# Attention and MLP on one core: the output block in consecutive rows, both squares of an MLP bank together, bulk loads issued in every step

## The chip, the cores and the metric

The kernel runs on one core of one Trainium2 chip. The time is the device time of one execution in microseconds (us). The core has five engines that run at the same time and wait for each other through semaphores: TensorE (PE, with PEld for its weight loads), VectorE (DVE), ScalarE (ACT), GpSimd (POOL) and SyncE (SP). In this kernel SP does nothing but issue DMA transfers, all of them, in the order in which the program lists them. Sixteen DMA engines move the bytes between the HBM and SBUF, the on-chip memory. TensorE writes its results to PSUM banks, from which ACT and DVE read.

## The reference

```python
def reference(A_x, A_wqkv, A_wo, B_x, B_w1, B_b1, B_w2, B_b2):
    xn = _layernorm(A_x, axis=-1)                     # (1, 2048, 640)
    s = _A_ref(xn, A_wqkv, A_wo)
    g = _silu(_B_ref(xn, B_w1, B_b1, B_w2, B_b2))
    return A_x + s * g

def _A_ref(x, wqkv, wo):                              # 32 heads of 20, window 256
    qkv = (x @ wqkv).reshape(B, S, 3, H, Dh).transpose(2, 0, 3, 1, 4)
    q, k, v = qkv[0], qkv[1], qkv[2]
    scores = jnp.einsum("bhqd,bhkd->bhqk", q, k) * (Dh ** -0.5)
    idx = jnp.arange(S)
    mask = (idx[:, None] - idx[None, :] >= 0) & (idx[:, None] - idx[None, :] < W)
    scores = jnp.where(mask[None, None], scores, -1e9)
    p = _softmax(scores, axis=-1)
    o = jnp.einsum("bhqk,bhkd->bhqd", p, v)
    return o.transpose(0, 2, 1, 3).reshape(B, S, D) @ wo

def _B_ref(x, w1, b1, w2, b2):                        # 640 -> 1536 -> 640
    h = jnp.einsum("bsd,df->bsf", x, w1) + b1
    r = jnp.where(h > 0, h, 0)
    return jnp.einsum("bsf,fd->bsd", r * r, w2) + b2
```

## The kernel before

**Precision.** A product of two float32 matrices is made of three: each operand is split into a high part, that TensorE takes at full rate, and the rest (`hi`, `lo`), and hi·hi, hi·lo and lo·hi are added up in one PSUM bank.

**Stages.** In the first stage (to about 115 us) the input is normalized, transposed and kept both in SBUF (`xT`) and in memory (`xs_d`); v and the first group of q and k are computed and stored (`v_d`, `qk_d`). The second stage is a loop over 16 head pairs times 16 tiles of 128 rows, plus 11 steps to run out: 267 steps. In step s, for pair p = s // 16 and tile q = s % 16, `scores` makes a tile of scores and `maxima` takes its row maxima on DVE. Every fourth step (s % 4 = 0) `max_rows` transposes the maxima of four tiles, ACT and POOL turn them into two rows, and SP sends these to rows 60 and 61 of the `qs` tile (L503), from where they are subtracted inside the next product. Nine steps behind (`LAG`), `scores_t` makes the transposed scores with these rows (`stps`, L518), ACT takes the exponential, POOL masks. Eleven steps behind, `values` multiplies four tiles by v (`ops`, L546), whose 21st column is all ones and so gives the sum of the row; ACT copies the result to `osb` (L551), and SP stores it to `o_d` (128 KB: for each of two heads and for even and odd tiles 32 rows, of which 21 are used, by two tiles of 128 columns).

**The filler.** The attention leaves TensorE time in each step. It is filled by a generator, `filler`: the other groups of q and k (`qkps`), then the MLP in eight blocks (two halves of the hidden width times four blocks of 512 rows), each with a first product (`hps`) and a second (`yps`). The order on every engine is written out by the program at build time. It keeps a planner's clock: `fill(upto)` emits filler work until the clock reaches its share of the step (`pace`), `later(wait, fn)` emits `fn` when the clock is `wait` on, and a bank released by `ps.free(after)` counts as free `after` later. `room()` lets the filler pause when no bank will be free in time.

**The MLP's evacuation.** Of a first-product bank (512 columns, two halves) ACT takes ReLU and Square of both halves (`hh`, the high part). `rest(i)` then makes the exact square of half i on DVE (`sq`, L936) and the low part on POOL (`hl`, L937). After the second one the bank is freed and the pair counts as made, so the second product may use it.

**Bulk loads.** The loads of the next head pair (`pair_loads`: eight of 240 KB, queued in the third and the tenth step of a pair) and of the next activation block (`load_xb`: ten of 256 KB) stand in a list. Twice a step `issue(RATE)` gives 0.9 of credit: raw weight pieces are started at 1.0 each, then listed loads at the cost that they were listed with (0.7 and 0.8). Credit does not add up beyond 0.9, but a debt is carried on. In steps with s % 4 = 3, and in steps with s % 4 = 0 until the maxima are out (`rowed`), `issue` returns at once. What a block needs and has not been started is started when the block begins (`ensure_bulk`).

**The closing stage** (`out_filler`, from about 794 us). For each of eight units u of 256 rows, `load(u)` brings the sums (`sums`), the attention's output (`ob`) and the MLP's rows (`yb`) back; `turn_out` takes the reciprocal of the sums, multiplies and splits; TensorE multiplies by wo (`wops`); DVE multiplies by the MLP's rows (`res`, L1098), POOL adds the input (L1103), and SP stores. In memory `o_d[g]` is addressed as row r (of 64), head h, column n before.

Of the kernel before, what the change touches and what calls it, by code (L numbers as in the profile page):

```python
# [9 lines left out]
F32 = mybir.dt.float32  # L10
# [5 lines left out]
P = 128  # L16
# [3 lines left out]
H = 32  # L20
# [37 lines left out]
def attn_mlp_kernel(ctx: ExitStack, tc, x, wqkv, wo, w1, b1, w2, b2, out):  # L58
# [23 lines left out]
        return [(dst[:, twice, :], f32(hi).unsqueeze(1).to_broadcast([P, 2, hi.shape[-1]])), (dst[:, once, :], f32(lo))]  # L82
    v_d = dram.tile([P, NP, NB, 4 * 2 * VW], F32, name="v_d")
    y_d = [dram.tile([P, NT, D], F32, name=f"y{i}") for i in range(2)]
    o_d = [dram.tile([2 * 32, H, MT], F32, name=f"o_{g}") for g in range(NB)]

# [443 lines left out]
    def values(p, g):  # L532
        for kb in range(4 * g, 4 * g + 4):
            pt = pts.pop((p, kb))
            ts = range(kb, min(kb + 3, NT))
            same, other = [t for t in ts if t % 2 == kb % 2], [t for t in ts if t % 2 != kb % 2]
            parts = [same] if kb % 8 < 6 else [[t] for t in same]
            for part in parts + [other]:
                for hh in range(2):
                    if not part:  # L540
                        continue
                    t = part[0]
                    r0 = 32 * (2 * hh + t % 2)
                    c0 = t // 2 % 4
                    first = t % 8 < 2 and kb == max(0, t - 2) or kb == 0
                    nc.tensor.matmul(ot[r0:r0 + VW, c0:c0 + len(part), :], vps[p][:, kb // 4, kb % 4, hh, :], pt[:, hh, :].rearrange("p (t n) -> p t n", n=P)[:, t - kb:part[-1] - kb + 1:2, :], start=first, stop=part[0] == kb, skip_group_check=True)  # L546
        clock[:2] = [max(clock[:2]) + PV] * 2

        def evac():
            osb = at2.tile([P, 2, P], F32, tag="osb", name="osb")  # L550
            nc.scalar.activation(osb, ot[:, 2 * g % 4:2 * g % 4 + 2, :], AF.Copy)  # L551
            post(o_d[g][:, 2 * p:2 * p + 2, :].rearrange("r h n -> h r n"), osb.rearrange("p e n -> p (e n)"))
        later(SOON, evac)


# [3 lines left out]
    def post(dst, src):  # L559
        posts.append((dst, src))  # L560
# [104 lines left out]
        return tiles[t][:, o:o + n]  # L665


    bulk, rowed = [], [False]
    credit = [0.0]

    def issue(amount):
        if state[2] % 4 == 3 or state[2] % 4 == 0 and not rowed[0]:
            return
        credit[0] = min(credit[0] + amount, amount)
        while credit[0] > 0 and start_pieces(1):
            credit[0] -= 1.0
        while bulk and credit[0] > 0:
            cost, fn = bulk.pop(0)
            fn()
            credit[0] -= cost  # L680
# [142 lines left out]
    def load_xb(b):  # L823
        xb = [bigp.tile([P, KC * BT], F32R, tag="big", name=f"xb{p}_{b}") for p in range(2)]
        cs = [slice(c * BT, (c + 1) * BT) for c in range(KC)]
        its = [bulk_dma(0.8, f32(xb[p])[:, c], xs_d[p][b][:, c]) for p in range(2) for c in cs]
        return xb, its

    def filler():
# [64 lines left out]
        for n, (hf, b) in enumerate(blocks):  # L894
# [20 lines left out]
            for th in range(2):  # L915
                for fp in range(NFH // 2):
                    yield from room()
                    ps = Acc(BT, "hps")

                    def evac(ps=ps, th=th, fp=fp, fi=hf * NFH + 2 * fp, hs=hs, made=made):  # L920
                        hh = [stg.tile([P, BT], F32R, tag="stg", name="hh"),
                              stg.tile([P, BT], F32R, tag="stg", name="hl") if fp == 0 else wgt.tile([P, D], F32R, tag=f"wg{'kq'[fp % 2]}l", name="hl")[:, :BT]]
                        hs[th, fp] = hh

                        vload[0] += 1.0
                        sls = [slice(i * MT, (i + 1) * MT) for i in range(2)]
                        rs = []
                        for i, sl in enumerate(sls):
                            rs.append(at2.tile([P, MT], F32, tag="relu", name="relu"))
                            nc.scalar.activation(rs[i], ps.tile[:, sl], AF.Relu, bias=b1t[:, fi + i:fi + i + 1])  # L930
                        for sl, r in zip(sls, rs):
                            nc.scalar.activation(hh[0][:, sl], r, AF.Square)  # L932

                        def rest(i):
                            sq = at2.tile([P, MT], F32, tag="sq", name="sq")
                            nc.vector.scalar_tensor_tensor(sq, ps.tile[:, sls[i]], b1t[:, fi + i:fi + i + 1], rs[i], ALU.add, ALU.mult)  # L936
                            nc.gpsimd.tensor_sub(hh[1][:, sls[i]], sq, f32(hh[0][:, sls[i]]))  # L937
                            if i:
                                made.add((th, fp))
                                ps.free(0.7)  # L940
                        later(0.6, lambda: rest(0))
                        later(1.0, lambda: rest(1))
                    job = open_job(evac, *([used] if (th, fp) == (1, NFH // 2 - 1) else []))
                    mms = [(i, lin1(wt1, (wp * KC + c) * FHALF + (2 * fp + i) * P, P), xb[xp][:, c * BT + th * MT:c * BT + (th + 1) * MT]) for i in range(2) for c in range(KC) for wp, xp in ((0, 0), (0, 1), (1, 0))]
                    for m, (i, w_, x_) in enumerate(mms):
                        halves(job, ps, w_, x_, m == 0, m == len(mms) - 1, i * MT, MT)
                        yield 0.1065
# [69 lines left out]
    def load(u):  # L1017
        if u in ld or u >= 2 * NB or not ready(u):
            return
        if u % 2 == 0:  # L1020
            obs[u // 2] = [bigp.tile([P, KC * BT], F32, tag="big", name=f"{w}_{u // 2}") for w in ("ob", "yb")]
        ob, yb = (t_[:, u % 2 * 2 * D:(u % 2 + 1) * 2 * D] for t_ in obs[u // 2])
        ob, yb = ob.rearrange("p (c n) -> p c n", c=KC), yb.rearrange("p (t d) -> p t d", t=2)
        sums = at2.tile([P, MT], F32, tag="sums", name="sums")
        rows = o_d[u // 2][32 * (u % 2):32 * (u % 2 + 1)]
        nc.sync.dma_start(sums, rows[DH].unsqueeze(0).to_broadcast([4, H, MT]))
        nc.sync.dma_start(ob, rows[:DH].rearrange("(c k) h n -> (k h) c n", k=4))
        t = tile_of(u, 0)
        nc.sync.dma_start(yb, y_d[1][:, t:t + 3:2, :])
        ld[u] = (ob, yb, sums)  # L1030
# [94 lines left out]
    with tc.manual_schedule(engines={E_.PE, E_.Activation, E_.DVE, E_.Pool, E_.SP}):  # L1125
        load_v(0)
        nc.vector.memset(ot, 0.0)
        loads = []

        def at_step(n):  # L1130
            return divmod(n, NT) if 0 <= n < NP * NT else None

        for s in range(steps):
            state[2], rowed[0] = s, False
            vload[0] = 0.2 * (s % 4 == 0) + 0.5 * (s % 4 == 3)
            post_all()
            issue(RATE)
            a, b, e = (at_step(s - lag) for lag in (0, LAG, LAG + PLAG))
            if a:
                p, q = a  # L1140
                if q == 0:
                    ensure_bulk(loads)
                if s == 2:
                    ones_rows(1)
                if q == 2 and p < NP - 1:
                    loads = [bulk_dma(0.7, *l) for l in pair_loads(p + 1, 0)]
                if q == LAG and p < NP - 1:
                    loads += [bulk_dma(0.7, *l) for l in pair_loads(p + 1, 1)]
                if q == LAG + 4 and p < NP - 1:
                    load_v(p + 1)  # L1150
            rows = None
            if a:
                sc = scores(p, q)
            if b:
                stp = scores_t(*b)
            if s % 4 == 0 and 0 < s <= NP * NT:
                rows = max_rows((s - 1) // NT, (s - 1) % NT // 4, stp[0] if b else pair_tile())
            if a:
                maxima(*a, *sc)
            if b:  # L1160
                exps(*b, *stp)
            if rows:
                rows()
            rowed[0] = True
            fill((s + EARLY_FILL) * pace)
            post_all()
            issue(RATE)
            flush()
            tick()
            if e and e[1] % 4 == 3:  # L1170
                fill((s + 1) * pace - PV)
                values(e[0], e[1] // 4)
            else:
                fill((s + 1) * pace)
        finish()
        state[2] = 10 ** 6
        for _ in fl:
            post_all()
            flush(mark() - 1)
        flush()  # L1180
        post_all()
# [23 lines left out]
```

## Time and profile before

| | |
|---|---|
| median of 3 runs | 875.52 us (875.32 to 877.31) |
| profiled execution | 873.83 us, span 872.1 us |
| TensorE busy | 853.6 us (98%) |
| DVE, ACT, POOL busy | 497.1, 401.0, 332.0 us |
| moved by DMA | 168.60 MB, mean 193 GB/s |
| stages | to 115 us preparation; 115 to about 794 the loop with the filler; then the closing stage |

The profile is of one execution. Its views used below: the page with each engine's busy time; windows, a row for each stretch of time (its length, then busy time of PE, PEld, DVE, ACT and POOL with the number of instructions, the granted clock as a share, the busy share of the DMA engines, and GB/s); waits (who waited for whom, us in total, times, the longest); the timeline (start, duration, engine, line, operation, out<-in, in brackets the idle time ahead of it and who ended it); and the chain of waits, followed back from the end. "L936" is line 936 of the kernel; an entry "SPq" is SP's queue issuing a transfer, and its duration is that of the issue, not of the transfer.

### The profile page before, as it was taken

The numbers are of one execution on the slowest core, as the hardware profiler recorded it, in microseconds if no ns is written. First come the engines' busy times: TensorE is split into PE (matmuls) and PEld (weight loads), VectorE is DVE, ScalarE is ACT, GpSimd is POOL, SyncE is SP. The second block draws the span as 40 slices with busy tenths as digits, with TensorE's granted clock in tenths as the row PEclk, the third lists the DMA queues.
The fourth block names the chain that finished last, engine by engine and source line by source line (L and its number), as shares of the span: only waits on it lengthen the run. The fifth ranks groups of instructions, "written<-read, shape, count | busy, mean of one in ns | idle before, by whom it ended". The sixth has DMA issues, their size and how long they took to land.

```text
span 872.1 us, 26728 instructions
## 1 busy us (share of the span) xinstructions
PE 853.6 (98%) x10640; PEld 796.5 (91%) x10640; DVE 497.1 (57%) x1448; ACT 401.0 (46%) x800; POOL 332.0 (38%) x700
## 2 busy tenths in 40 slices
PE   9999999999999999999999999999999999999998
PEld 8999999888888999989989989998989999999998
DVE  7652146656567755555655566764655555536764
ACT  5222114545556744644644654743643644653231
POOL 6010002333333643643543543642543543541343
PEclk9999999999999999999999999999999999999999
DMA  7997578787788546245348346367348256157995
GB/s 268 310 399 276 173 205 264 252 256 232 256 275 287 128 144 177 70 138 187 78 129 249 85 114 182 98 196 214 85 129 244 81 148 200 50 163 236 288 296 172
DMA packets 92901, 168.60 MB, mean 193 GB/s; under 512 B 9448, under 2 KB 41320, under 8 KB 91752
## 3 DMA queue, kind: packets, MB, share of 16 engines
q1 hardware_dynamic: 92776, 166.89, 62.1%
q8 instruction: 84, 1.38, 0.7%
q14 instruction: 41, 0.34, 0.1%
HBM read 94.71 MB, written 71.57 MB: 191 GB/s over the span
## 4 chain that ended last, share of the span: by engine, by line
PE 86%; DMA 7%; DVE 2%; issue 2%; ACT 1%; POOL 1%; SPq 0%; DVEq 0%; POOLq 0%; ACTq 0%
PE yps L468 19%; PE hps L468 18%; PE qkps L468 13%; PE ops L546 9%; PE vps L228 8%; PE stps L518 5%; PE wops L599 4%; PE sps L478 4%; DMA qs<-mrow 4%; PE qkps L205 3%; DMA out_dram<-res 2%; DMA vp<-v_d 1%; POOL res L1103 1%; PE tps L172 1%; DVE junk L486 0%
## 5 line engine op out<-in xcount | busy, mean ns | idle before, releaser
L486 DVE CUSTOM_DVE_ANT_0 junk<-sps,mask 128x384 bf16<-128x384 f32 (+2 forms) x512 | 272.3, 532 | 211.4 <-PE sps L478 57.6
L524 ACT ACTIVATE p<-stps 128x768 f32<-128x768 f32 (+2 forms) x256 | 197.8, 773 | 291.8 <-PE stps L518 240.9
L468 PE MATMUL yps<-w,hh 64*128 64x320 f32 x1536 | 229.3, 310 | 5.1 <-DVE sq L936 4.7
L525 POOL TENSOR_SCALAR_AFFINE_SELECT p<-p 128x256 f32<-128x256 f32 x256 | 105.9, 414 | 333.0 <-ACT p L524 329.8
L468 PE MATMUL hps<-xb,w 64*128 64x256 f32 x2520 | 218.5, 284 | 0.0
L468 PEld LDWEIGHTS hps<-xb,w 64*128 64x128 f32 x2520 | 207.0, 188 | 5.5 <-issue 5.4
L468 PEld LDWEIGHTS yps<-w,hh 64*128 64x128 f32 x1536 | 181.5, 185 | 11.3 <-DVE sq L936 6.2
L468 PE MATMUL yps<-w,hl 64*128 64x320 f32 x768 | 172.4, 309 | 0.0
L478 PE MATMUL sps<-ks,qs 60*128 60x384 f32 (+2 forms) x512 | 140.9, 342 | 0.8 <-DVE mt L486 0.5
L518 PE MATMUL stps<-qs,ks 62*128 62x384 f32 (+2 forms) x512 | 132.8, 334 | 4.9 <-DMA qs<-mrow 4.8
L468 PEld LDWEIGHTS yps<-w,hl 64*128 64x128 f32 x768 | 112.3, 185 | 1.8 <-issue 1.7
L468 PE MATMUL qkps<-xT,wgkh 64*128 64x512 f32 x320 | 100.9, 395 | 0.0
L468 PE MATMUL qkps<-xT,wgqh 64*128 64x512 f32 x320 | 99.2, 393 | 0.0
L546 PE MATMUL ops<-p,vp 128*21 128x128 f32 (+1 forms) x2112 | 92.8, 313 | 0.0
L527 POOL TENSOR_SCALAR_AFFINE_SELECT p<-p 128x256 f32<-128x256 f32 x224 | 92.7, 414 | 0.0
L518 PEld LDWEIGHTS stps<-qs,ks 62*128 62x128 f32 x512 | 85.8, 188 | 7.4 <-issue 7.0
L478 PEld LDWEIGHTS sps<-ks,qs 60*128 60x128 f32 x512 | 86.0, 186 | 2.9 <-DVE mt L486 1.7
L546 PEld LDWEIGHTS ops<-p,vp 128*21 128x21 f32 x2112 | 65.2, 100 | 22.0 <-issue 8.8
L937 POOL TENSOR_TENSOR hl<-sq,hh 128x256 fp32r<-128x256 f32 x96 | 71.0, 756 | 24.5 <-ACT hh L932 21.9
L228 PE MATMUL vps<-wv,xT 128*128 128x320 f32 x480 | 71.5, 308 | 0.0
L228 PEld LDWEIGHTS vps<-wv,xT 128*128 128x128 f32 x480 | 70.5, 188 | 0.1
L599 PE MATMUL wops<-wo,oT 128*128 128x320 f32 x384 | 63.2, 314 | 2.1 <-DVE res L1098 1.4
(100 smaller groups left out, 1188.0 us busy)
## 6 DMA issues: line engine op xcount, KB each, us to landing
ks<-k_d SPq DMA_DIRECT2D x64, 240.0 KB
qs<-q_d SPq DMA_DIRECT2D x64, 240.0 KB
xb<-xs SPq DMA_DIRECT2D x60, 256.0 KB
xs<-xT SPq DMA_DIRECT2D x8, 1280.0 KB
y<-ysb SPq DMA_DIRECT2D x32, 320.0 KB
k_d<-shm SPq DMA_DIRECT2D x19, 512.0 KB
q_d<-shm SPq DMA_DIRECT2D x19, 512.0 KB
o<-osb SPq DMA_DIRECT2D x64, 128.0 KB
```

What stands on the lines that cost most here:

```text
L205: nc.tensor.matmul(ps, wt[:, c, :], xT[part][b][:, c * BT + t0:c * BT + t0 + n], start=m == 1, stop=m == 3 * KC)
L228: nc.tensor.matmul(ps, xT[xp][b][:, c * BT + t * P: c * BT + (t + 1) * P], wv[wp][:, c, nh * HALF:(nh + 1) * HALF], start=first and m == 0 ...
L468: return nc.tensor.matmul(out, a[r], b_[r], skip_group_check=True, **kw)
L478: nc.tensor.matmul(ss[hh][:, :nk], qs[i][o, q * P:(q + 1) * P], ks[i][o, k0 * P:k0 * P + nk], start=True, stop=True)
L486: nc.vector.tensor_tensor_reduce(out=junk[:, :nk], in0=ss[hh][:, :nk], in1=mask[:, 3 * P - nk:], scale=1.0, scalar=-3.0e38, op0=ALU.add, o ...
L518: nc.tensor.matmul(tps[:, hh, :n], ks[i][o, kb * P:(kb + 1) * P], qs[i][o, kb * P:kb * P + n], start=True, stop=True)
L524: nc.scalar.activation(p32[:, :, :n], tps[:, :, :n], AF.Exp, scale=SCALE)
L525: nc.gpsimd.affine_select(p32[:, :, 0:P], p32[:, :, 0:P], pattern=[[0, 2], [1, P]], compare_op=ALU.is_ge, fill=0.0, base=0, channel_multip ...
L527: nc.gpsimd.affine_select(p32[:, :, 2 * P:], p32[:, :, 2 * P:], pattern=[[0, 2], [-1, P]], compare_op=ALU.is_gt, fill=0.0, base=0, channel ...
L546: nc.tensor.matmul(ot[r0:r0 + VW, c0:c0 + len(part), :], vps[p][:, kb // 4, kb % 4, hh, :], pt[:, hh, :].rearrange("p (t n) -> p t n", n=P ...
L599: nc.tensor.matmul(ps, a, b_, start=j == 0, stop=j == n - 1)
L937: nc.gpsimd.tensor_sub(hh[1][:, sls[i]], sq, f32(hh[0][:, sls[i]]))
```

## The change

There are three edits.

1. `o_d[g]` becomes 16 pairs by 128 partitions by 256 columns, so a block of `osb` goes to 128 consecutive rows (128 KB in one piece). Loading it back needs the head and the row taken apart again: for each k of 4, one transfer for the sums to 32 partitions and one for the output rows k, k + 4, ... to the same 32 partitions; nine issues for a unit with the MLP's rows, where there were three.
2. `issue` returns early in no step, and `rowed` is gone; a load of an activation block costs 0.4 of credit instead of 0.8.
3. Both halves' `rest` run in one go, 0.8 after the evacuation instead of 0.6 and 1.0; the bank counts as free 1.0 after that instead of 0.7.

```diff
-    o_d = [dram.tile([2 * 32, H, MT], F32, name=f"o_{g}") for g in range(NB)]
+    o_d = [dram.tile([NP, P, MT], F32, name=f"o_{g}") for g in range(NB)]
...
-            post(o_d[g][:, 2 * p:2 * p + 2, :].rearrange("r h n -> h r n"), osb.rearrange("p e n -> p (e n)"))
+            post(o_d[g][p], osb.rearrange("p e n -> p (e n)"))
...
-    bulk, rowed = [], [False]
+    bulk = []
     credit = [0.0]

     def issue(amount):
-        if state[2] % 4 == 3 or state[2] % 4 == 0 and not rowed[0]:
-            return
         credit[0] = min(credit[0] + amount, amount)
...
-        its = [bulk_dma(0.8, f32(xb[p])[:, c], xs_d[p][b][:, c]) for p in range(2) for c in cs]
+        its = [bulk_dma(0.4, f32(xb[p])[:, c], xs_d[p][b][:, c]) for p in range(2) for c in cs]
...
                             if i:
                                 made.add((th, fp))
-                                ps.free(0.7)
-                        later(0.6, lambda: rest(0))
-                        later(1.0, lambda: rest(1))
+                                ps.free(1.0)
+                        later(0.8, lambda: (rest(0), rest(1)))
...
-        rows = o_d[u // 2][32 * (u % 2):32 * (u % 2 + 1)]
-        nc.sync.dma_start(sums, rows[DH].unsqueeze(0).to_broadcast([4, H, MT]))
-        nc.sync.dma_start(ob, rows[:DH].rearrange("(c k) h n -> (k h) c n", k=4))
+        rows = o_d[u // 2].rearrange("p (h r) n -> (p h) r n", h=2)[:, 32 * (u % 2):32 * (u % 2) + VW]
+        for k in range(4):
+            nc.sync.dma_start(sums[32 * k:32 * k + H], rows[:, DH])
+            nc.sync.dma_start(ob[32 * k:32 * k + H], rows[:, k:DH:4])
...
-            state[2], rowed[0] = s, False
+            state[2] = s
...
-            rowed[0] = True
```

## The prediction

> **What bounds the kernel now.** I read the page first, then the busy time by stage, then the waits of TensorE between 115 and 794 us, and last the single places where it waits.
>
> ```profile
> span 872.1 us, 26728 instructions
> PE   853.6 (98%) x10640; PEld 796.5 (91%) x10640; DVE 497.1 (57%) x1448; ACT 401.0 (46%) x800; POOL 332.0 (38%) x700
> ```
> ```profile
> 270.00:410.00 140.00, 137.96 (x2104) 128.97 (x2106) 82.99 (x273) 73.37 (x153) 65.23 (x144) 1.00 0.53 156
> 410.00:540.00 130.00, 126.76 (x1941) 118.70 (x1940) 77.01 (x254) 68.89 (x146) 58.53 (x132) 1.00 0.47 136
> 540.00:680.00 140.00, 136.18 (x2066) 127.36 (x2064) 81.74 (x266) 72.39 (x153) 64.16 (x141) 0.99 0.57 163
> 794.00:872.10 78.10, 72.94 (x480) 71.95 (x480) 49.24 (x69) 18.50 (x21) 30.10 (x30) 0.98 0.82 254
> ```
> TensorE does the same matmuls before and after, so the change can only win idle time or cost some: 872.1 - 853.6 = 18.5 us in all. The three middle rows hold 2.0 + 3.2 + 3.8 = 9.1 us of it, the closing stage 5.2 us. The clock is full throughout, and the DMA engines are half idle in the middle (0.47 to 0.57) but not at the end (0.82).
>
> ```profile
> PE stps L518 <- DMA qs<-mrow: 4.8, 6, 1.6
> PE yps L468 <- DVE sq L936: 4.7, 5, 1.3
> PE sps L478 <- DVE mt L486: 0.5, 2, 0.4
> ```
> ```profile
> PEld stps L518 <- issue: 7.0, 8, 1.8
> ```
> (Who waits, for whom: us in total, times, the longest.) The named waits in that stretch are two. Six times the transposed scores wait for the row maxima that travel from SBUF to the qs tile by DMA (4.8 us; the weight loads show eight such places, 7.0 us). Five times the second MLP product waits for the second square, which empties a PSUM bank (4.7 us). Both are what the change touches.
>
> **Row maxima and the output block.** One of the six waits, in the chain of waits:
>
> ```profile
> 216.23 0.51 SPq L503
> ...
> 216.84 6.14 DMA qs<-mrow
> ...
> 223.11 0.44 PE stps L518 x2
> ```
> The second maxima transfer is issued at 216.84 and lands 6.14 us later; the matmul starts 0.13 us after that. So 6.3 us from issue to use is all the room there is. What is in front of such a transfer is seen in the SP queue before another of the six:
>
> ```profile
> 330.75 0.40 SPq L683 DMA_DIRECT2D ks<-k_d  x1
> ...
> 332.08 0.40 SPq L683 DMA_DIRECT2D qs<-q_d  x1
> 334.18 0.53 SPq L564 DMA_DIRECT2D o<-osb  x1
> ...
> 336.26 1.12 SPq L503 DMA_DIRECT2D qs<-mrow  x2
> 337.48 0.36 SPq L683 DMA_DIRECT2D ks<-k_d  x1
> ```
> Four pair loads, then the hold (no bulk load until the maxima are out), and 2.1 us ahead of the maxima the store of an output block. That store is slow by itself. A stretch in which it runs nearly alone, and a store of 160 KB over 128 consecutive rows at the very end:
>
> ```profile
> q1 hardware_dynamic: 150, 0.14, 9.5%
> ...
> o<-osb SPq DMA_DIRECT2D x1, 128.0 KB
> qs<-mrow SPq DMA_DIRECT2D x2, 4.0 KB
> ```
> ```profile
> 762.50:763.00 0.50, 0.50 (x11) 0.50 (x9) 0.00 (x0) 0.49 (x3) 0.50 (x2) 1.00 0.14 49
> ```
> ```profile
> 870.40:870.90 0.50, 0.00 (x0) 0.00 (x0) 0.00 (x0) 0.00 (x0) 0.00 (x0) 1.00 0.86 300
> ```
> In the two rows of windows the last columns are clock, share of the DMA engines, GB/s. The output block moves at 49 GB/s with 0.14 of the engines busy, which is two of sixteen (0.125); the other store moves at 300 GB/s with 0.86 busy. At 49 GB/s, 131 kB take 2.7 us on two engines; at 300 GB/s they take 0.4 us on all. The old destination is a pattern of 2 heads by 64 rows, the new one 128 consecutive rows like the 160 KB store. I expect the new one to run like that store: 2.7 - 0.4 = 2.3 us less in front of whatever comes next on those two engines. No row tells on which engines the maxima travel; their destination is again 2 heads by a row. Bounds: if on others, nothing is won (0); if on the same two, each of the waits (longest 1.8) goes, 7.0 us. I take **-5.0 us**, near the 4.8 that matmuls show, since the maxima's own pattern is nearest to the block's.
>
> The Trainium skill, "DMA: Bandwidth & Descriptors", section "Why a DMA increments its semaphore by 16 and not by 1", says that a transfer is spread over the largest number of engines up to 16 that divides the outermost size of both sides, and takes the lowest-numbered ones. By it the old block (2 x 64) and the maxima (2 x ...) share the same two engines, and the new block has all; the 0.14 above agrees. By the rule alone the sum would have -7.0 in place of -5.0.
>
> **Bulk loads not held, and activation blocks at half the cost.** The step length follows from the maxima, two transfers every four steps:
>
> ```profile
> L503 SPq DMA_DIRECT2D qs<-mrow x128: 496/508/1653, 127.3 to 762.0; - x128
> ```
> (762.0 - 127.3) / 63 / 4 = 2.52 us. The maxima go out in steps 0 mod 4. Of eight issue calls in four steps, three were skipped before (both of step 3, the first of step 0) and none now. A pair load costs 0.7 of a credit of 0.9, so four of them go out as 2, 1, 1: queued in the third step of a head pair, two went before the maxima and two after; now all four go before. When the DMA engines are full they move
>
> ```profile
> 594.00:596.00 2.00, 2.00 (x30) 2.00 (x28) 1.55 (x5) 1.09 (x2) 0.67 (x2) 1.00 0.98 282
> ```
> 282 GB/s, so 2 x 246 kB more in front are 1.7 us, less than the 2.3 freed; and these maxima (group 0) have five steps to their first use, not three. The second batch of pair loads (tenth step) meets no hold. The six loads of an activation block are ten transfers of 262 kB at 0.4 instead of 0.8: 2.25 a call instead of 1.1, all out in 4.4 calls or 5.6 us, where they need 2.6 MB / 282 GB/s = 9.3 us. The backlog at the end is 3.7 us; less 2.3 leaves 1.4 us on the maxima that follow, six times at worst: 8.4 us. Against that, what is sent sooner is not in front later: in the rows above the four pair loads were pushed to just ahead of the maxima because activation loads at 0.8 stood before them. Bounds -2 (two of the eight places) to +8.4; I take **+1.0 us**, nearer the low end, because most bursts will not end on a maxima step (one step in four).
>
> **Both squares together.** One of the five waits:
>
> ```profile
> 304.70 0.49 DVE L936 SCALAR_TENSOR_TENSOR sq<-hps,b1t,relu 128x256 f32<-128x256 f32 x1 [0.96 <-ACT relu L930]
> ...
> 305.19 0.56 DVE L486 CUSTOM_DVE_ANT_0 junk<-sps,mask 128x384 bf16<-128x384 f32 x1
> ...
> 305.90 0.56 DVE L486 CUSTOM_DVE_ANT_0 junk<-sps,mask 128x384 bf16<-128x384 f32 x1
> ...
> 306.39 0.48 DVE L936 SCALAR_TENSOR_TENSOR sq<-hps,b1t,relu 128x256 f32<-128x256 f32 x1
> ...
> 306.92 0.41 PE L468 MATMUL yps<-w,hh 64*128 64x320 f32 x1 [0.65 <-DVE sq L936]
> ```
> No instruction is added. At 0.6 and 1.0 of the planner's clock the squares stand on both sides of two maxima; at 0.8 both stand on one side. In front: the second ends at 305.7, 1.2 us earlier, and this wait of 0.65 is gone, while the maxima start 0.5 us later (the wait of scores for maxima is 0.5 us in all, so there is room). Behind: the second ends where it does now, nothing is won. So -4.7 to 0 for the five waits; the bank is promised at 0.8 + 1.0 = 1.8 instead of 1.7 after the evacuation, which moves some matmuls behind by the planner's own reckoning: I allow +1.5. I take **-1.5 us**, a third of the waits.
>
> **Loading the output back.** Per block of 256 rows, one transfer for the sums and one for the output become four and four; with the MLP's rows, 9 issues for 3.
>
> ```profile
> 774.67 1.78 SPq L751 DMA_DIRECT2D raw<-in_A_wo_dram  x3
> ...
> 834.86 0.53 SPq L1026 DMA_DIRECT2D sums<-o  x1
> ...
> 836.06 0.66 SPq L1029 DMA_DIRECT2D yb<-y  x1
> 841.06 0.35 SPq L1063 DMA_DIRECT2D xres<-in_A_x_dram  x1
> ```
> ```profile
> 840.89 1.74 DVE L1040 RECIPROCAL sums<-sums 128x256 f32<-128x256 f32 x1
> ```
> ```profile
> DVE res L1098 <- DMA out_dram<-res: 9.6, 6, 4.2
> ...
> PE wops L599 <- DVE res L1098: 1.4, 3, 0.8
> ```
> The nearest row for a 32-row transfer is the wo weight: three in 1.78 us, 0.59 each. Six more are 3.5 us: SP, done at 836.7, would be done at 840.2, before the next issue at 841.06, so no queue behind it is held. The last sums transfer goes out 3.5 us later and the reciprocal runs 6.0 us after the first: it has to land in 2.5 us. The bytes are the same, and the sums, now read with an outermost size of 4, would be spread wider and land sooner each; VectorE has some play, since it waits 9.6 us for res buffers and only 1.4 us of that reaches TensorE. Bounds: -1.4 (that wait goes) and the rival below; I take **0**.
>
> The sum: -5.0 + 1.0 - 1.5 + 0 = **-5.5 us**, from the profiled execution's 873.83 us to 868.3. The median of the runs, 875.52, stands 1.7 above the profiled one: **870.0 us**.
>
> **Rivals.**
> 1. Slower, by bulk in front of the maxima. If the block's store was not what delays them, the freed 2.3 us is nothing to them, and the two extra loads put 1.7 us on each row. It decides once issue to landing exceeds 6.3 us. For it: SP itself waits for old transfers,
>
> ```profile
> SPq L503 <- DMA vp<-v_d: 1.1, 1, 1.1
> ```
> so more loads in flight hold the maxima's issue too. Price: eight places x 1.7 = 13.6, less 1.5 for the squares: about 887 us; with half the places 881. Against it: 0.14 and 49 GB/s.
> 2. Slower, by the closing stage. The last sums land as long after their issue as now (up to 6.0 us), the reciprocal is 3.5 us late in each of seven blocks and the products behind it on VectorE too; if half reaches TensorE, 12 us: 870 + 12 = 882. For it: 0.82 of the DMA engines busy. Against: SP's room and the shorter queue. The Trainium skill, same page, section "Rules for kernel authors", advises one 128-partition transfer over pieces in partition halves and calls transfers under 64 KB mostly overhead, some 2 us fixed; by it the 32 KB sums pieces cost more than the one they replace. The three issues in 1.78 us show that such pieces overlap at least in issue.
> 3. No change: the maxima arrive earlier, but other waits take the place (backlogs of activation loads, banks promised 0.1 later), or store and maxima never met: 875 us. For it: the waits at stake are 1% of the span.
>
> **Chances and range.** The forecast 0.60, rival 3 0.20, rival 1 0.12, rival 2 0.08. A measurement tells about 0.3% (2.6 us) from no change: faster is below 872.9, slower above 878.1. The forecast's own range is 862 (7.0, 4.7 and 1.4 all won, from 875.5) to 872.9. The whole range takes in rival 3 and the lower part of 1 and 2: 862 to 881.
>
> **What would show it.** In the new profile: the output block's store with a share of the engines far over 0.14; no stps wait on qs<-mrow; two sq side by side on VectorE and the yps wait on sq below 3 us; SP in the closing stage done before the next xres. The prediction is wrong if maxima waits remain or grow, if the second product waits for something in their place, or if the closing stage is longer than 78 us.

## The result, and the profile after

The changed kernel takes 878.81 us (median of 20 runs), the kernel before 874.61 us in its 20 runs: a ratio of 1.0044, 95% interval 1.0032 to 1.0056. It is slower by 0.4%, where 870 us was forecast. The profiled execution took 876.63 us, with a span of 874.9 us against 872.1.

The page of the changed kernel:

```profile
span 874.9 us, 26825 instructions
...
PE 853.3 (98%) x10640; PEld 795.5 (91%) x10640; DVE 499.0 (57%) x1448; ACT 400.9 (46%) x800; POOL 330.1 (38%) x700
```

The work is the same (10640 matmuls; TensorE is busy for 853.3 us, before for 853.6), so what grew is the time in which TensorE is idle: 874.9 - 853.3 = 21.6 us, before 18.5. The waits of TensorE between 115 and 794 us:

```profile
PE yps L468 <- DVE ysb L965: 6.5, 3, 5.9
PE sps L478 <- DVE mt L486: 2.1, 5, 1.2
PE yps L468 <- DVE sq L934: 1.9, 5, 0.7
```

The line that stood first before, `stps` waiting for the maxima (4.8 us), is gone. The waits for squares fell from 4.7 to 1.9 us, those of the scores for maxima on DVE rose from 0.5 to 2.1. New is one wait of 5.9 us for an evacuation of the second MLP product (`ysb`).

Where on the way it happens can be read from two tiles. Of the instructions on `stps` (the transposed scores) and on `wops` (the products with wo), the view gives the number, the least, median and longest duration in ns, and the start of the first and the last. Before:

```profile
L518 PE MATMUL stps<-qs,ks x512: 220/336/518, 138.4 to 778.8; 62*128 62x384 f32 x150, 62*128 62x128 f32 x11, 62*128 62x256 f32 x10
L599 PE MATMUL wops<-wo,oT x384: 302/309/468, 794.1 to 867.7; 128*128 128x320 f32 x192
L599 PE MATMUL wops<-wo4h,oT x64: 308/309/468, 797.2 to 868.1; 128*128 128x320 f32 x64
```

After:

```profile
L518 PE MATMUL stps<-qs,ks x512: 218/336/443, 138.5 to 770.3; 62*128 62x384 f32 x150, 62*128 62x128 f32 x11, 62*128 62x256 f32 x10
L599 PE MATMUL wops<-wo,oT x384: 302/309/416, 795.0 to 870.5; 128*128 128x320 f32 x192
L599 PE MATMUL wops<-wo4h,oT x64: 309/309/313, 796.8 to 870.9; 128*128 128x320 f32 x64
```

Three sections follow from these starts: the loop to the last transposed scores, the handover from there to the first product with wo, and the closing stage from there to the last such product.

| us | loop, to | handover | closing stage | end |
|---|---|---|---|---|
| before | 778.8 | 15.3 | 74.0 | 868.1 |
| after | 770.3 | 24.7 | 75.9 | 870.9 |
| difference | -8.5 | +9.4 | +1.9 | +2.8 |

So the loop gained more than forecast, and the gain was given back at the handover and, for a smaller part, in the closing stage.

The store of an output block, nearly alone, in the changed kernel (length of the stretch, busy time of the five engines, clock, DMA share, GB/s); before, the last two were 0.14 and 49 GB/s:

```profile
750.50:751.00 0.50, 0.50 (x12) 0.50 (x11) 0.00 (x0) 0.30 (x1) 0.00 (x0) 1.00 0.72 242
```

The handover, VectorE's timeline (start, duration, engine, line, what, and the idle time ahead with who ended it), and TensorE's beside it:

```profile
773.71 0.49 DVE L965 TENSOR_TENSOR ysb<-yps,yin 128x320 f32<-128x320 f32 x1 [2.15 <-PE yps L468]
...
778.47 0.82 DVE L774 TENSOR_TENSOR wo4l<-raw,wo4h 128x640 fp32r<-128x640 f32 x1 [2.81 <-ACT wo4h L773]
779.21 1.74 DVE L1038 RECIPROCAL sums<-sums 128x256 f32<-128x256 f32 x1
...
784.85 0.96 DVE L109 TENSOR_TENSOR oT<-ob,oT 128x768 fp32r<-128x768 f32 x1 [0.91 <-ACT oT L108]
785.72 0.88 DVE L965 TENSOR_TENSOR ysb<-yps,yin 128x320 f32<-128x320 f32 x2
```
```profile
780.04 0.31 PE L468 MATMUL yps<-w,hl 64*128 64x320 f32 x1
786.26 0.90 PE L468 MATMUL yps<-w,hh 64*128 64x320 f32 x4 [5.91 <-DVE ysb L965]
```

VectorE has a split of a piece of wo, a reciprocal and the whole normalization of the first unit (778.47 to 785.8) ahead of two evacuations. TensorE has filled its last free bank at 780.35 and waits for the first of them. In windows of the same stretch:

```profile
780.00:784.00 4.00, 0.35 (x3) 0.09 (x1) 3.21 (x4) 0.66 (x2) 0.00 (x0) 1.00 0.65 173
784.00:788.00 4.00, 1.74 (x12) 1.74 (x14) 1.76 (x3) 3.37 (x3) 0.00 (x0) 0.53 0.63 220
788.00:792.00 4.00, 3.90 (x30) 3.61 (x29) 0.49 (x1) 0.00 (x0) 0.00 (x0) 0.62 0.37 113
792.00:796.00 4.00, 3.33 (x23) 3.09 (x23) 1.64 (x2) 0.00 (x0) 0.00 (x0) 1.00 0.08 28
```

The wait costs more than its 5.9 us: TensorE comes back to a granted clock of 0.53 and 0.62.

Before, the same normalization stood at the same place, and VectorE was just as long at it:

```profile
784.10 0.49 DVE L968 TENSOR_TENSOR ysb<-yps,yin 128x320 f32<-128x320 f32 x1 [2.15 <-PE yps L468]
784.51 0.82 DVE L776 TENSOR_TENSOR wo4l<-raw,wo4h 128x640 fp32r<-128x640 f32 x1
785.24 1.75 DVE L1040 RECIPROCAL sums<-sums 128x256 f32<-128x256 f32 x1
...
791.76 0.88 DVE L968 TENSOR_TENSOR ysb<-yps,yin 128x320 f32<-128x320 f32 x2
```

But one evacuation more was already done (three left, four after), so TensorE had one bank more to write to. The planner's own state, read while the program is built, says the same. At the start of each of the last two products of the last MLP block it stands at (step, planner's clock, evacuations due but not written out, free banks):

```
            before                              after
product 6   step 265  640.83  due 0  free 1     step 266  641.82  due 0  free 1
product 7   loop over 645.44  due 0  free 1     loop over 646.44  due 1  free 0
```

The filler is 0.99 behind on the planner's clock. When product 7 starts behind the loop, an evacuation is due and not written out, and `late`, which then writes out the wo split and the first unit's normalization, does so ahead of it.

### The profile page after: what moved, and what is told of

The parts are those of the page before. It is cut to its first block, busy times and chain, and to the rows that moved or that the text cites. A ratio compares the mean times of both kernels' runs of the same rounds, so it can differ in the third digit from the quotient of the medians.

```text
span 874.9 us, 26825 instructions
## 1 busy us (share of the span) xinstructions
PE 853.3 (98%) x10640; PEld 795.5 (91%) x10640; DVE 499.0 (57%) x1448; ACT 400.9 (46%) x800; POOL 330.1 (38%) x700
## 4 chain that ended last, share of the span: by engine, by line
PE 87%; DMA 4%; DVE 3%; issue 2%; ACT 1%; POOL 1%; SPq 0%; DVEq 0%; POOLq 0%; ACTq 0%
PE hps L468 20%; PE yps L468 19%; PE qkps L468 14%; PE ops L546 10%; PE vps L228 8%; PE stps L518 5%; PE sps L478 5%; PE qkps L205 3%; DMA out_dram<-res 3%; PE wops L599 2%; POOL res L1101 1%; DVE junk L486 1%; PE tps L172 1%; DMA sums<-o 1%; DMA yb<-y 1%
## 5 line engine op out<-in xcount | busy, mean ns | idle before, releaser
L468 PE MATMUL yps<-w,hh 64*128 64x320 f32 x1536 | 233.2, 313 | 8.7 <-DVE ysb L965 6.5
L468 PEld LDWEIGHTS yps<-w,hh 64*128 64x128 f32 x1536 | 186.3, 187 | 15.0 <-DVE ysb L965 8.0
L468 PE MATMUL yps<-w,hl 64*128 64x320 f32 x768 | 175.8, 311 | 0.0
L478 PE MATMUL sps<-ks,qs 60*128 60x384 f32 (+2 forms) x512 | 144.2, 342 | 2.3 <-DVE mt L486 2.1
L518 PE MATMUL stps<-qs,ks 62*128 62x384 f32 (+2 forms) x512 | 136.8, 331 | 0.0
L468 PEld LDWEIGHTS yps<-w,hl 64*128 64x128 f32 x768 | 116.1, 187 | 1.7 <-issue 1.7
L478 PEld LDWEIGHTS sps<-ks,qs 60*128 60x128 f32 x512 | 87.8, 185 | 5.7 <-DVE mt L486 4.2
L518 PEld LDWEIGHTS stps<-qs,ks 62*128 62x128 f32 x512 | 88.3, 187 | 0.4
```

The costliest lines, as they stand in the source:

```text
L468: return nc.tensor.matmul(out, a[r], b_[r], skip_group_check=True, **kw)
L478: nc.tensor.matmul(ss[hh][:, :nk], qs[i][o, q * P:(q + 1) * P], ks[i][o, k0 * P:k0 * P + nk], start=True, stop=True)
L518: nc.tensor.matmul(tps[:, hh, :n], ks[i][o, kb * P:(kb + 1) * P], qs[i][o, kb * P:kb * P + n], start=True, stop=True)
```

## The experiments

Theory A: the squares' edit shifts the planner's clock by a little, so the handover finds no free bank; layout and no hold are gains in the loop. Rival B: the nine issues for a unit cost the time in the closing stage. Rival C: bulk loads in front of the maxima cost it. Each ratio below is to the kernel before, measured beside the run.

**e1, the layout and its loads back alone.**

```diff
+    o_d = [dram.tile([NP, P, MT], F32, name=f"o_{g}") for g in range(NB)]
...
+            post(o_d[g][p], osb.rearrange("p e n -> p (e n)"))
...
+        rows = o_d[u // 2].rearrange("p (h r) n -> (p h) r n", h=2)[:, 32 * (u % 2):32 * (u % 2) + VW]
+        for k in range(4):
+            nc.sync.dma_start(sums[32 * k:32 * k + H], rows[:, DH])
+            nc.sync.dma_start(ob[32 * k:32 * k + H], rows[:, k:DH:4])
```

> The kernel before with the output block's layout (and its loads back) alone. Theory A (the squares' edit moves the planner's clock so that at the handover to the closing stage TensorE runs out of banks): no handover wait here, the maxima waits gone, the closing stage perhaps 2 us longer: 868 to 871 us. Rival B (the nine issues for a unit in the closing stage are what costs): not below 874. In the trace, A: stps waits on qs<-mrow near 0, no yps wait on ysb over 1 us.

869.52 us, ratio 0.9947 (0.9924 to 0.997).

**e2, e1 and bulk loads not held**, squares as before.

```diff
     def issue(amount):
-        if state[2] % 4 == 3 or state[2] % 4 == 0 and not rowed[0]:
-            return
...
+        its = [bulk_dma(0.4, f32(xb[p])[:, c], xs_d[p][b][:, c]) for p in range(2) for c in cs]
```

> Layout and bulk loads not held, squares as before. Theory A: within 1.5 us of the layout alone, 868 to 871 us. Rival C (bulk loads not held put traffic in front of what TensorE needs): 3 us or more above the layout alone.

869.57 us, ratio 0.9946 (0.9926 to 0.9966). Both lie where A put them. TensorE's waits in e1:

```profile
PE wops L599 <- DVE res L1099: 5.8, 9, 1.1
PE yps L468 <- DVE sq L936: 4.7, 5, 1.3
```

There is no wait for the maxima, and at the handover only one of 0.7 us, which the kernel before has too. But B is not wrong either: in the closing stage TensorE waits 5.8 us for DVE, where it was 1.4.

**e3, the squares alone.**

```diff
-                                ps.free(0.7)
-                        later(0.6, lambda: rest(0))
-                        later(1.0, lambda: rest(1))
+                                ps.free(1.0)
+                        later(0.8, lambda: (rest(0), rest(1)))
```

> The kernel before with the squares' edit alone. Theory A: the handover wait of about 6 us and a low granted clock after it are here, the maxima waits (about 5 us) stay, the waits for squares shrink by 2 to 3 us: 879 to 883 us. Rivals B and C: 871 to 874 us, since neither the loads back nor the hold is touched.

885.77 us, ratio 1.0136 (1.011 to 1.0163): more than A expected, and far from B and C. The profile is of its fastest execution, 881.7 us.

```profile
PE yps L468 <- DVE ysb L967: 7.2, 3, 6.6
PE stps L518 <- DMA qs<-mrow: 5.7, 7, 1.8
PE yps L468 <- DVE sq L936: 1.9, 5, 0.7
PE sps L478 <- DVE mt L486: 1.9, 4, 1.2
```

**e4, the changed kernel with what is due written out first.**

```diff
             if state[2] < 10 ** 6:
                 return
+            finish()
             start_pieces()
```

> The changed kernel with one line more: once the loop is over, evacuations that are due are written out before the wo split and the first unit's normalization. Theory A: the ysb wait of 5.9 us is gone, and so is most of the low clock behind it: 868 to 871 us. Rivals B and C: 876 us or more, since layout, loads and hold are as in the changed kernel.

870.92 us, ratio 0.9963 (0.9947 to 0.998). One line that adds no work, but changes an order, brings the ratio from 1.0044 to 0.9963. (Its profile is of its fastest execution, 867.45 us.) The same place, now at 778 to 790 us:

```profile
778.00:782.00 4.00, 4.00 (x54) 3.82 (x52) 3.27 (x4) 0.63 (x1) 0.00 (x0) 1.00 0.47 143
782.00:786.00 4.00, 3.53 (x27) 3.00 (x23) 3.09 (x6) 2.53 (x3) 0.00 (x0) 1.00 0.83 249
786.00:790.00 4.00, 3.39 (x23) 3.42 (x24) 3.22 (x5) 1.49 (x2) 0.00 (x0) 1.00 0.88 277
```

TensorE is idle for 1.1 us in these three windows (6.7 us in the four above), and the clock stays full.

**e5, the old addresses and the old loads back, but the store cut in two**, one transfer of 64 rows for each head; no hold, squares as before. It asks whether the scattered rows or the outermost size made the store slow, and gives the closing stage its three issues again.

```diff
-            post(o_d[g][:, 2 * p:2 * p + 2, :].rearrange("r h n -> h r n"), osb.rearrange("p e n -> p (e n)"))
+            for h in range(2):
+                post(o_d[g][:, 2 * p + h, :], osb[h * HP:(h + 1) * HP].rearrange("p e n -> p (e n)"))
```

> The old address order of the output block, loads back in three issues as before, squares as before, bulk loads not held; the block's store is cut into two transfers of 64 rows, one for each head. Theory D (the store was slow because its outermost size is 2, not because the rows are apart; and the loads back in nine issues cost the closing stage 4 us): the maxima waits are gone as with the new layout, the closing stage takes 74 us instead of 78, the whole 864 to 867 us. Rival E (it is the scattered rows that are slow): maxima waits of 4 us or more remain, 873 us or more.

864.98 us, ratio 0.9881 (0.9849 to 0.9914): faster than both kernels. Of the maxima waits 0.9 us is left:

```profile
PE yps L468 <- DVE sq L935: 4.8, 5, 1.3
PE wops L600 <- DVE res L1097: 1.4, 3, 0.8
PE stps L518 <- DMA qs<-mrow: 0.9, 1, 0.9
```

So the rows may lie apart: with the addresses unchanged, an outermost size of 64 in place of 2 takes the waits away.

**e6, bulk loads not held alone** (the diff of e2 on the kernel before, with the slow store kept).

> The kernel before with bulk loads not held, and nothing else. Theory D: the slow store is still in front of the maxima and more loads with it, so the waits of stps for maxima grow from 4.8 us: 875 to 879 us. Rival F (the hold never mattered, what is sent sooner is out of the way): within 1 us of before, or faster.

874.78 us, ratio 1.0005 (0.9981 to 1.0029). The waits for the maxima grow from 4.8 to 6.1 us, the longest from 1.6 to 2.8, as D said, but the time does not move beyond the interval: F by the time, D by the trace.

```profile
PE stps L518 <- DMA qs<-mrow: 6.1, 5, 2.8
```

**e7, as e2 with both squares at 0.8 and the bank free 0.9 later** (1.7 after the evacuation as before, 1.8 in the change).

```diff
-                                ps.free(1.0)
+                                ps.free(0.9)
                         later(0.8, lambda: (rest(0), rest(1)))
```

> Layout and no hold; both squares at 0.8 as in the change, but the bank counts as free 0.9 later, so at 1.7 after the evacuation as before (1.8 in the change). Theory A with the planner tipped by the squares being together: the handover wait of some 6 us is there, 876 to 880 us. If the later bank time alone tips it: no such wait, 868 to 871 us.

880.21 us, ratio 1.0051 (1.0023 to 1.0079), at the upper end of what A gave.

```profile
PE yps L468 <- DVE ysb L965: 5.4, 2, 5.0
PE yps L468 <- DVE sq L934: 5.0, 7, 1.3
```

The wait for `ysb` at the handover (5.0 us) is there. So the later bank is not needed for it: the squares together are enough to tip the planner. The second line says something else: with the squares together and the bank as before, the waits for squares are 5.0 us, not less than the 4.7 before. The 1.9 us of e3 and of the changed kernel came only with the bank that is promised 0.1 later.

**e8, as e2 with seven issues for a unit**, all of 128 partitions. The rows of wo are loaded in the order that matches.

```diff
-        for k in range(4):
-            nc.sync.dma_start(sums[32 * k:32 * k + H], rows[:, DH])
-            nc.sync.dma_start(ob[32 * k:32 * k + H], rows[:, k:DH:4])
+        nc.sync.dma_start(sums, rows[:, DH].unsqueeze(1).to_broadcast([H, 4, MT]))
+        for c in range(KC):
+            nc.sync.dma_start(ob[:, c], rows[:, 4 * c:4 * c + 4])
```

> Layout and no hold, squares as before, but the unit is loaded with seven issues of 128 partitions (sums once, output in five, MLP rows; the rows of wo are ordered to match, which makes one transfer of four there). Theory D, that the number of issues and their being 32 partitions wide cost 4 us in the closing stage: 76 us or less there, 866 to 868 us. If it is the new address order itself: 78 us as with nine issues, 869 to 870 us.

867.54 us, ratio 0.9916 (0.9885 to 0.9948). The closing stage takes 74.9 us where e2's took 78.9.

**e9, e5 with the squares together and what is due written out first.**

> The split store of e5 with the squares together and the evacuations due written out first at the handover. If the squares edit is worth something once its handover wait is away, this is 862 us or less; if, as the last transposed scores of e2 and the changed kernel suggest (769.6 and 770.3 us), it only moves the waits from the squares to the maxima, 864 to 867 us.

864.92 us, ratio 0.9895 (0.9871 to 0.9919), the same as e5 (0.9881) within the intervals. With the handover mended, the squares edit is worth nothing in the time. In its profiled execution the loop ends 2.5 us sooner than in e5, and the handover and the closing stage give it back.

The sections of all profiled executions, from the first and last starts as above; the first column is the start of the first transposed scores:

| us | loop, from | loop, to | handover | closing stage |
|---|---|---|---|---|
| before | 138.4 | 778.8 | 15.3 | 74.0 |
| e1 layout | 140.1 | 770.9 | 15.3 | 78.4 |
| e2 layout, no hold | 138.6 | 769.6 | 15.2 | 78.9 |
| e3 squares | 138.6 | 778.7 | 24.7 | 72.6 |
| after (all three) | 138.5 | 770.3 | 24.7 | 75.9 |
| e4 after, due first | 138.5 | 769.8 | 16.8 | 75.1 |
| e5 split store, no hold | 138.6 | 770.9 | 15.2 | 73.0 |
| e6 no hold | 138.7 | 780.1 | 15.3 | 73.8 |
| e7 squares, bank early | 138.5 | 769.5 | 27.0 | 79.5 |
| e8 seven issues | 138.6 | 769.5 | 15.3 | 74.9 |
| e9 e5, squares, due first | 138.4 | 768.4 | 16.9 | 75.3 |

Each row is one execution, so a difference of a microsecond or two between rows may be that execution's own. The long handover is not: TensorE's mean granted clock, recorded for each of these executions, lies between 0.988 and 0.996 in all of the changed kernel, e3 and e7, and at 0.998 or more in all of e1, e2, e5, e8 and e9; the kernel before, e4 and e6 spread from 0.993 to 1.0.

## Why the prediction was wrong

The forecast was a gain of 5.5 us; the median moved by +4.2. Term by term:

- **Row maxima and the output block (-5.0): right in the mechanism, too small in size.** The store runs at 242 GB/s instead of 49, and no wait of `stps` for the maxima is left. With the layout alone the loop takes 630.8 us instead of 640.4 (first to last start), 9.6 us less, where 7.0 was taken as the best case. The 7.0 us of the weight loads are gone. What the prediction left out is the clock: it called it full throughout, but its own rows show 0.99 and 0.98, and behind the longest wait for the maxima (1.6 us, to 605.4) the kernel before has

```profile
606.00:610.00 4.00, 4.00 (x44) 3.91 (x43) 0.94 (x3) 1.59 (x3) 0.77 (x2) 0.58 0.54 150
```

  which e1 does not have. At half the clock for 3.4 of these 4 us, TensorE does 1.7 us less work (an estimate from the 0.58). The rest of the 9.6 us is not accounted for. The cause of the slow store was shown by e5: with the old addresses and 64 rows as the outermost size, nearly the whole gain is there. By the Trainium skill's rule ("DMA: Bandwidth & Descriptors", "Why a DMA increments its semaphore by 16 and not by 1") 64 rows spread over 16 engines and 2 heads over two; e5 agrees (0.9 us of the 4.8 are left). That the maxima share those two engines was inferred before and is still not seen on a row; that they land in time once the store is off them is.
- **Bulk loads not held (+1.0): nothing.** With the fast store the loop takes as long as without the edit (630.8 us in e1, 631.0 in e2), and the medians are the same. With the slow store it takes 1.0 us more (641.4 in e6, 640.4 before), by single executions, and the median does not move beyond its interval. Rival 1 of the prediction has its mechanism shown in e6, at a price that does not count.
- **Both squares together (-1.5, bounds -4.7 to +1.5): this step failed.** In the loop, the waits for squares shrank by as much as was forecast (4.7 to 1.9), but not for the reason given: e7, with the squares together and the old bank time, still has 5.0, so that this number came out was luck. 1.6 us came back as scores waiting for maxima on DVE (0.5 to 2.1), for which the prediction saw room. Behind the longest of these (1.2 us, to 506.5) the changed kernel's clock was at half for some 3.4 us (0.88, 0.50, 0.50, 0.50, 0.91 in the windows of 1 us from 507 to 512); e4, with the same waits, kept it. Alone the edit moved the loop's end by 0.1 us (e3). What the prediction put down as "moves some matmuls behind by the planner's own reckoning: I allow +1.5" was where the loss lay, though it was put down to the later bank, and by e7 the squares together do it without that. The planner's clock is 0.99 late at the end of the loop, one evacuation is not written out when `late` starts on the wo split and the normalization, and the handover takes 9.4 us more. It was costed as a delay of some matmuls; it is a step that is taken or not, depending on where the loop ends between two products. e3 has it with the squares alone, e1 and e2 lack it, and e4 takes it away with the evacuation first.
- **Loading the output back (0): mis-sized, and rival 2 had it.** With the layout alone the closing stage grew by 4.4 us (74.0 to 78.4), and by 3.3 between e3 and the changed kernel, which share a handover. The prediction found room for nine issues of 0.59 us on SP. The issues took 0.3 to 0.6 us, most of them, but they did not follow each other. In e1, one unit (SP's timeline):

```profile
817.67 0.55 SPq L1064 DMA_DIRECT2D xres<-in_A_x_dram  x1
818.31 0.96 SPq L1027 DMA_DIRECT2D sums<-o  x1
...
822.93 0.31 SPq L1027 DMA_DIRECT2D sums<-o  x1
824.41 0.31 SPq L1028 DMA_DIRECT2D ob<-o  x1
824.77 0.44 SPq L1030 DMA_DIRECT2D yb<-y  x1
```
```profile
SPq L1028 <- DMA xres<-in_A_x_dram: 7.5, 7, 1.5
```

The last `ob` load has nothing to do with `xres`, but waits for it: xres at 817.67 is the eighth transfer ahead of it. The prediction's row "SPq L503 <- DMA vp<-v_d" was the same thing, read there only for the maxima: the load of v at 591.96 is the eighth transfer ahead of the second maxima transfer at 600.0, the one behind the wait of 1.6 us. With nine issues a unit, SP is held in this way in each of seven units of e1, and the MLP's rows go out 6.5 us after the first sums instead of 1.2 (834.86 to 836.06 before). The sums come late too: VectorE waits for them, as rival 2 said,

```profile
DVE sums L1041 <- DMA sums<-o: 3.7, 4, 1.7
```

  where it waited 0.2 us before. That TensorE's 5.8 us for `res` follow from this is argued, not shown. e8 with seven issues of 128 partitions takes back 4.0 of the 4.9 us between e2 and before, e5 with three all of them. Whether their number or their 32 partitions weigh more was not separated. The Trainium skill's advice against pieces in partition halves ("DMA: Bandwidth & Descriptors", "Rules for kernel authors") agrees with this (78.9 us with nine issues, 74.9 with seven of 128 partitions), though what the rows show is waits of issue and not the pieces' own duration.

The chances: rivals 1 and 2, the two ways to be slower, held 0.20 together, and rival 2's mechanism was the smaller part of the loss. The larger part is nearest to rival 3 (0.20): the maxima do arrive earlier, and another wait takes the place. But rival 3 named the later bank and saw no change, where the handover cost 9.4 us. That the whole range (862 to 881) holds the result is no credit to the mechanism. Of the signs that were named, the one on the second product ("waits for something in their place") came true; the closing stage over 78 us was no sign, since by the prediction's own row it had 78.1 before. The sum was made from rows of waits and left out that the order of the program itself has an edge.

## What to carry to other kernels

Where the order of all engines is written out by a planner, the cost of a shift of its clock does not follow from its size: look for the places where it decides an order (here, whether an evacuation goes ahead of a long block on the same engine), and make the order there explicit, as `finish()` does. Look at the outermost size of each transfer: one store of 2 heads by 64 rows was slow, two stores of 64 rows to the same addresses were fast. And when one transfer becomes several, count them against the transfers that are still in flight (here an issue waited for the eighth ahead of it), not against the issue time alone.

## What the runs showed of the hardware

In the changed kernel TensorE's granted clock fell by half at about 784.2 us (0.62 is the mean of that window), after 3.9 us of idle, and was full again at 791, 4.7 us after the matmuls had begun anew at 786.26 (windows of 1 us):

```profile
783.00:784.00 1.00, 0.00 (x0) 0.00 (x0) 0.94 (x2) 0.03 (x1) 0.00 (x0) 1.00 0.85 174
784.00:785.00 1.00, 0.00 (x0) 0.00 (x0) 0.15 (x1) 0.98 (x2) 0.00 (x0) 0.62 0.70 180
785.00:786.00 1.00, 0.00 (x0) 0.00 (x0) 1.00 (x2) 1.00 (x1) 0.00 (x0) 0.50 1.02 402
...
790.00:791.00 1.00, 1.00 (x12) 1.00 (x8) 0.00 (x0) 0.00 (x0) 0.00 (x0) 0.50 0.00 0
791.00:792.00 1.00, 0.90 (x8) 0.61 (x7) 0.49 (x1) 0.00 (x0) 0.00 (x0) 0.97 0.00 0
```

The Trainium skill ("TensorE: Matmul & The Clock Gate", "Part 1: The HAM clock gate (the "warmup" mystery)") says that an idle window of some 3.4 us halves the clock and that as long of sustained work restores it; this trace is near that. But the kernel before lost the clock after far shorter waits: behind the 1.6 us that end at 605.4 (the row for 606 to 610 shown with the row maxima), and at its handover, where TensorE had been idle for 0.7 us only (793.39 to 794.06):

```profile
792.00:796.00 4.00, 3.32 (x18) 3.09 (x17) 3.00 (x5) 1.42 (x2) 0.00 (x0) 0.79 1.03 333
796.00:800.00 4.00, 4.00 (x24) 4.00 (x23) 2.62 (x4) 1.06 (x2) 0.97 (x1) 0.78 0.91 279
```

Both times it was at half for about 3.4 us (worked out from the means). After the same 0.7 us at the handover, e1 and e2 kept the full clock. So here a wait of one or two microseconds could cost the clock as well, but did not always; what decides is open. In e7 the clock did not come back so soon:

```profile
786.00:788.00 2.00, 2.00 (x20) 2.00 (x18) 0.00 (x0) 0.54 (x1) 0.00 (x0) 0.50 0.71 207
...
794.00:796.00 2.00, 1.79 (x7) 1.39 (x6) 0.17 (x1) 0.00 (x0) 0.00 (x0) 0.50 0.00 0
...
800.00:802.00 2.00, 2.00 (x11) 2.00 (x10) 1.30 (x3) 0.00 (x0) 0.57 (x1) 0.61 0.93 210
```

There TensorE was busy from 785.4 on, with one gap of 0.7 us, and ran at half the clock until about 801.6 us. Its handover and closing stage together are 5.9 us longer than the changed kernel's (27.0 + 79.5 against 24.7 + 75.9). Why the low clock lasted three times as long is open.
